# dV of head pair 0: GpSimd's rows as 16 KB packets instead of 8 KB

## The chip, the cores and the metric

The kernel runs on one core of a Trainium2 chip. The metric is device time in microseconds (us). Before the change the median of three runs is 633.36 us (632.92 to 633.75). A profiled execution is a separate run, with its own time: 632.87 us.

## The reference: what is computed

Attention of one query row per head over 8192 keys, forward and backward, in bfloat16, for 32 heads of size 128:

```python
scores = einsum('bhqd,bhkd->bhqk', q, k) * Dh**-0.5     # B=1, H=32, Sq=1, Skv=8192, Dh=128
attn   = softmax(scores, axis=-1)
out    = einsum('bhqk,bhkd->bhqd', attn, v)
out, vjp = jax.vjp(that, q, k, v);  return out, *vjp(grad_out)
```

The outputs are `out` and `dq` (8 KB each), `dk` and `dv` (64 MB each). With one query row, dK is an outer product of the row dS and q, and dV of the row P and grad_out. K and V are read (134 MB), dK and dV written (134 MB).

## The kernel before, in words

The heads are taken two at a time: 16 pairs. A pair's K is a tile of 128 partitions (64 per head) by 128 slots by 128 elements: 32 KB in each partition, 4 MB in all, and the same for V. Partition p holds 128 consecutive rows of the sequence, so its 32 KB are contiguous in memory too. There are three buffers for K and two for V. dK and dV are written in place over K and V (`outer`, line 285, on the vector engine, in eight parts of 16 slots), and the tiles are then stored to `out_2` and `out_3`. A buffer is loaded again only when its store has landed.

The loop over j runs through the pairs. It finishes dK of pair j-1, makes the scores and the softmax of pair j, and writes dV of pair j; the order of the instructions on each engine is the program's (`tc.manual_schedule`).

All loads of K and V and nearly all stores are issued from SP's queue, in the program's order, one DMA of 128 partitions each, so that each of the 16 DMA engines gets 8 rows of it. Pair 0's V is the exception on the way out. Line 299 stores its upper 64 slots from SP. Its lower 64 slots (`SHARED = 64`; 128 rows of 16 KB, 2 MB) are stored from GpSimd's queue by `share_out` (line 115), as soon as the fourth part of dV is written (line 296). `share_out` cuts the 128 rows into six DMAs, listed in `SHARES` as (engine, first row, number of rows); each takes every third row from the first:

```python
SHARES = ((6, 12, 39), (5, 2, 42), (5, 1, 8), (15, 55, 25), (10, 25, 10), (7, 0, 4))
```

The program keeps a model of which DMA engine GpSimd's queue will begin with, `cursor`. Line 121 moves it on, after a DMA of n rows, by the largest divisor of n up to 16, as if a DMA of n rows is dealt in equal runs to that many consecutive engines. `turn_to` (line 105) issues a small DMA of a few bytes a row (`turned`, line 111) ahead of each of the six, to bring the cursor to the engine that `SHARES` names. By this model the 39 rows go three each to the 13 engines from 6 on (6 to 15, 0, 1, 2), the 42 rows three each to 14 engines from 5, the 8 rows one each to 8 engines from 5, the 25 rows five each to the 5 engines from 15, the 10 rows one each to 10 engines from 10, and the 4 rows one each to 4 engines from 7.

At the end of the program GpSimd's queue also stores the two small results (line 341): 32 rows of 256 B each.

Pair 0's V buffer is loaded with pair 2's V after both stores have landed (`load_v`, line 93).

Of the kernel before, what the change touches and what calls it, by code (L numbers as in the profile page):

```python
# [31 lines left out]
def kernel(  # L32
# [11 lines left out]
    nc = tc.nc  # L44
# [62 lines left out]
    def turn_to(engine):  # L107
        n = (engine - cursor[0]) % 16
        if n:
            rows = n if n > 1 else 17  # L110
            nc.gpsimd.dma_start(turned[0:rows, cursor[1]],  # L111
                                k[0, 0].rearrange("(p n) d -> p n d", p=P)[0:rows, 0:2, 0:2])
            cursor[1] += 1
        cursor[0] = engine

    def share_out(dst, src):
        for engine, first, n in SHARES:
            turn_to(engine)
            last = first + 3 * n - 2
            nc.gpsimd.dma_start(dst[first:last:3], src[first:last:3], max_dma_last_dim=8192)  # L120
            cursor[0] = (cursor[0] + max(i for i in range(1, 17) if n % i == 0)) % 16

    ident = consts.tile([P, P], BF16)
# [162 lines left out]
    def outer(j, which, r):  # L286
        x = st[j]
        G, dst = (Kt[j], out_2) if which == "dk" else (Vt[j], out_3)
        rep, row = x["ds"] if which == "dk" else x["p"], qd[j][:, 0 if which == "dk" else 1, :]
        nc.vector.tensor_tensor(  # L290
            slots(G, r, NU).rearrange("p n (a b) -> p n a b", b=R),
            slots(rep, r, NU).unsqueeze(2).to_broadcast([P, CH, D // R, R]),
            row.rearrange("p (a b) -> p a b", b=R).unsqueeze(1).to_broadcast([P, CH, D // R, R]),
            op=ALU.mult)
        if (which, j) == ("dv", 0):
            if (r + 1) * CH == SHARED:
                share_out(rows_of(dst, 0)[:, 0:SHARED, :], G[:, 0:SHARED, :])
            elif r == NU - 1:
                nc.sync.dma_start(rows_of(dst, 0)[:, SHARED:NT, :], G[:, SHARED:NT, :])
            return  # L300
        ends = ENDS.get((which, j), (8,))
        if r + 1 in ends:
            i = ends.index(r + 1)
            a, b = (ends[i - 1] if i else 0) * CH, (r + 1) * CH
            nc.sync.dma_start(rows_of(dst, j)[:, a:b, :], G[:, a:b, :])
# [49 lines left out]
    for j in range(HP + 1):  # L355
# [30 lines left out]
        if j == 0:  # L386
            blocks(1)
            first = psT.tile([P, 512], F32, tag="T", name="first")
# [136 lines left out]
```

## Time and profile before

| | |
|---|---|
| median of three runs | 633.36 us (632.92 to 633.75) |
| profiled execution, its own time | 632.87 us |
| its span, first to last instruction | 631.1 us |
| vector engine busy | 516.4 us (82%) |
| TensorE busy | 462.9 us (73%) |
| moved by DMA | 268.98 MB in 12164 packets, mean 426 GB/s |
| GpSimd's queue (q0) | 800 packets, 2.12 MB |
| SP's queue (q1) | 11232 packets, 266.34 MB |

The profile is one execution. Times in it are in microseconds from the start of the span. A packet is one contiguous piece that one DMA engine moves; each of the 16 engines moves its packets one after the other. The trace holds for each packet its queue, start, duration and size, but not the number of its engine. "DMA share" is the mean busy share of the 16 engines; it can be a little over 1, since one packet's record begins some nanoseconds before the record of the packet ahead of it ends.

### The profile page before, as it was taken

What the parts mean: (1) busy time and instruction counts of PE and PEld (TensorE: products, weight loads), DVE (VectorE), ACT (ScalarE), POOL (GpSimd) and SP (SyncE); (2) the same over time, 40 slices, a digit from 0 to 9 for tenths busy, and PEclk for the clock granted to TensorE, in tenths of its full rate; (3) what the DMA queues carried; (4) which work ended last, traced back from release to release, by engine and by line L of the source; (5) the groups of instructions that cost most, each with busy time, mean ns of one, the idle gap of its engine ahead of it and who ended that gap; (6) DMA issues with size and microseconds to landing.
All of it is one profiled execution on the core that took longest, in us unless ns stands there. A gap on an engine that the chain in (4) does not pass through costs nothing.

```text
span 631.1 us, 8018 instructions
## 1 busy us (share of the span) xinstructions
PE 462.9 (73%) x3256; PEld 245.9 (39%) x3256; DVE 516.4 (82%) x654; ACT 205.1 (32%) x460; POOL 11.3 (2%) x23
## 2 busy tenths in 40 slices
PE   4887678878787788676888757867679776697671
PEld 1443344244443425233363432624336243262441
DVE  6579997989889798796879959879697895987973
ACT  2432424043342505134052330613316142160431
POOL 2040000000000000000000000000000000000000
PEclk9789987789798977788868789777897778987785
DMA  8999999999999999999999999999999999999997
GB/s 366 433 402 436 430 428 431 429 427 440 433 427 436 436 431 433 433 432 429 429 432 429 427 433 427 433 432 418 431 430 437 436 431 425 436 427 431 428 426 336
DMA packets 12164, 268.98 MB, mean 426 GB/s; under 512 B 1856, under 2 KB 1888, under 8 KB 1888
## 3 DMA queue, kind: packets, MB, share of 16 engines
q1 hardware_dynamic: 11232, 266.34, 98.5%
q0 software_dynamic: 800, 2.12, 0.8%
q8 instruction: 25, 0.41, 0.2%
q14 instruction: 11, 0.09, 0.0%
q10 hardware_dynamic: 96, 0.02, 0.0%
HBM read 134.23 MB, written 134.23 MB: 425 GB/s over the span
## 4 chain that ended last, share of the span: by engine, by line
issue 91%; DMA 3%; PE 3%; DVE 1%; ACT 0%; POOL 0%; POOLq 0%; ACTq 0%
DMA out_dram<-Vt 2%; PE s_ps L198 1%; DMA Kt<-in_k_dram 1%; PE T_ps L215 1%; PE acc_p L265 0%; DVE XK_sb L188 0%; DVE Vt L290 0%; POOL out_dram L120 0%; DVE q_blk L174 0%; ACT p_rep L452 0%; DVE sT L205 0%; ACT win L255 0%; ACT e L440 0%; POOL turned L111 0%; POOLq L520 0%
## 5 line engine op out<-in xcount | busy, mean ns | idle before, releaser
L198 PE MATMUL s_ps<-XK_sb,q_win 128*128 128x512 bf16 x512 | 152.4, 432 | 66.6 <-DVE XK_sb L188 61.3
L290 DVE TENSOR_TENSOR Vt<-p_rep,qd 128x2048 bf16<-128x2048 bf16 x128 | 154.0, 1223 | 40.1 <-PE acc_p L265 32.2
L188 DVE STREAM_TRANSPOSE XK_sb<-Kt 128x1024 f32<-128x1024 f32 x128 | 150.2, 1218 | 37.7 <-DMA Kt<-in_k_dram 35.0
L215 PE MATMUL T_ps<-ident_f,Vt 128*128 128x128 f32 x1024 | 165.4, 314 | 6.1 <-DMA Vt<-in_v_dram 6.1
L220 ACT COPY XV_sb<-T_ps 128x512 f32<-128x512 f32 x256 | 139.6, 591 | 82.6 <-PE T_ps L215 82.4
L290 DVE TENSOR_TENSOR Kt<-ds_rep,qd 128x2048 bf16<-128x2048 bf16 x128 | 149.5, 1215 | 3.2 <-PE acc_ds L265 2.8
L215 PEld LDWEIGHTS T_ps<-ident_f,Vt 128*128 128x128 f32 x1024 | 131.2, 160 | 43.8 <-issue 18.7
L198 PEld LDWEIGHTS <-q_win 128*128 128x128 bf16 x512 | 51.6, 110 | 155.6 <-issue 123.9
L265 PE MATMUL acc_p<-Vt,win 128*32 128x512 bf16 x512 | 55.9, 439 | 2.8 <-ACT win L255 2.8
L440 ACT ACTIVATE e<-sT,nbias 128x128 f32<-128x128 f32 x16 | 8.2, 515 | 150.6 <-DVE nbias L436 150.6
L265 PEld LDWEIGHTS <-win 128*32 128x32 bf16 x1024 | 23.0, 99 | 60.6 <-issue 49.4
L265 PE MATMUL acc_ds<-Kt,win 128*32 128x512 bf16 x512 | 42.7, 429 | 4.6 <-ACT win L255 4.6
L232 PE MATMUL dp_ps<-XV_sb,do_win 128*32 128x512 bf16 x512 | 34.3, 383 | 13.5 <-ACT XV_sb L220 13.5
L255 ACT COPY win<-ds 64x128 bf16<-64x128 bf16 x32 | 9.5, 296 | 106.4 <-DVE ds L327 106.2
L232 PEld LDWEIGHTS <-do_win 128*32 128x32 bf16 x512 | 14.3, 94 | 29.2 <-issue 22.5
L441 PE MATMUL m_ps<-rs,ones_f 128*128 128x1 f32 x32 | 7.5, 305 | 24.4 <-ACT e L440 24.4
L427 PE MATMUL m_ps<-ident_f,top 128*128 128x128 f32 x16 | 4.8, 300 | 23.5 <-DVE top L425 23.5
L205 DVE STREAM_TRANSPOSE sT<-s_ps 128x512 f32<-128x512 f32 x16 | 11.5, 717 | 10.7 <-PE s_ps L198 10.7
L441 PEld LDWEIGHTS m_ps<-rs,ones_f 128*128 128x128 f32 x32 | 6.2, 242 | 27.6 <-ACT e L440 27.6
L452 ACT ACTIVATE p_rep<-e,rinv 128x512 bf16<-128x512 f32 x16 | 11.5, 722 | 13.3 <-DVE rinv L450 13.3
L427 PEld LDWEIGHTS m_ps<-ident_f,top 128*128 128x128 f32 x16 | 2.1, 133 | 31.0 <-issue 25.4
L317 PEld LDWEIGHTS m_ps<-pd,ones_f 128*128 128x128 f32 x32 | 8.2, 276 | 10.6 <-DVE prod L248 9.8
(60 smaller groups left out, 158.1 us busy)
## 6 DMA issues: line engine op xcount, KB each, us to landing
Kt<-in_k_dram SPq DMA_DIRECT2D x14, 4096.0 KB, 29.1
Vt<-in_v_dram SPq DMA_DIRECT2D x14, 4096.0 KB, 29.0
out_dram<-Kt SPq DMA_DIRECT2D x13, 4096.0 KB, 25.1
out_dram<-Vt SPq DMA_DIRECT2D x13, 4096.0 KB, 32.3
out_dram<-Vt SPq DMA_DIRECT2D x5, 2048.0 KB, 16.2
out_dram<-Kt SPq DMA_DIRECT2D x5, 2048.0 KB, 15.7
Kt<-in_k_dram SPq DMA_DIRECT2D x4, 1024.0 KB, 8.2
Vt<-in_v_dram SPq DMA_DIRECT2D x2, 2048.0 KB, 17.5
```

What stands on the lines that cost most here:

```text
L188: nc.vector.transpose(XK[j, u][:].rearrange("p g w i -> p (g w i)"), slots(Kt[j], u, NU).rearrange("p g d -> p (g d)").bitcast(F32))
L198: nc.tensor.matmul(st[j]["s"][:], lhsT=q_win[:, c, at:at + P], rhs=cols[:, c // 2, c % 2], start=(u == 0 and c == 0), stop=(u == NU - 1 an ...
L205: nc.vector.transpose(sT[:].rearrange("p g r -> p (g r)"), x["s"][:])
L215: nc.tensor.transpose(T_ps[:, i, :], words[:, m * P:(m + 1) * P], ident_f[:])
L220: nc.scalar.copy(XV[j][:, b * TB:(b + 1) * TB, :], st[j].pop(("T", c))[:])
L232: nc.tensor.matmul(out[b * QD:(b + 1) * QD, :], lhsT=do_win[:, b // 2, e2, at:at + QD], rhs=cols[:, z, e2, :, b * QD:(b + 1) * QD], start= ...
L255: nc.scalar.copy(win[t * M:(t + 1) * M, :, at:at + 4], src[t * M:(t + 1) * M])
L265: nc.tensor.matmul(acc[which][b * QD:(b + 1) * QD, :], lhsT=win[:, g, at:at + QD], rhs=X[:, 4 * g:4 * g + 4, :].rearrange("p n d -> p (n d)"),
L290: nc.vector.tensor_tensor(slots(G, r, NU).rearrange("p n (a b) -> p n a b", b=R), slots(rep, r, NU).unsqueeze(2).to_broadcast([P, CH, D // ...
L317: nc.tensor.matmul(x["m"][:, 1:3], lhsT=ones_f[:], rhs=x["pd"][:], start=True, stop=True, skip_group_check=True)
L441: nc.tensor.matmul(x["m"][:, 0:1], lhsT=ones_f[:], rhs=rs[:], start=True, stop=True, skip_group_check=True)
L452: nc.scalar.activation(x["p"][:], e[:].unsqueeze(2).to_broadcast([P, NT, R]), ACT.Copy, scale=rinv[:])
```

## The change

The limit on the contiguous piece that one packet of `share_out`'s DMAs may carry goes from 8192 to 16384 bytes. A row has 16384 bytes. In the program before, the access pattern of such a DMA is n rows by 2 pieces by 4096 elements; it becomes n rows by 8192 elements.

```diff
         for engine, first, n in SHARES:
             turn_to(engine)
             last = first + 3 * n - 2
-            nc.gpsimd.dma_start(dst[first:last:3], src[first:last:3], max_dma_last_dim=8192)
+            nc.gpsimd.dma_start(dst[first:last:3], src[first:last:3], max_dma_last_dim=16384)
             cursor[0] = (cursor[0] + max(i for i in range(1, 17) if n % i == 0)) % 16
```

`SHARES`, `turn_to` and the arithmetic on `cursor` stay as they are.

## The prediction

> **What bounds the kernel now.** I read the page's head first. No engine is busy all the time (vector engine 82%), and the chain that ended last is 91% "issue", so it names no cause. Then the DMA lines:
>
> ```profile
> DMA  8999999999999999999999999999999999999997
> GB/s 366 433 402 436 430 428 431 429 427 440 433 427 436 436 431 433 433 432 429 429 432 429 427 433 427 433 432 418 431 430 437 436 431 425 436 427 431 428 426 336
> q1 hardware_dynamic: 11232, 266.34, 98.5%
> q0 software_dynamic: 800, 2.12, 0.8%
> q8 instruction: 25, 0.41, 0.2%
> ```
>
> The 16 DMA engines are the bound: 98.5% and 0.8% of their time is spent on packets. Next the table by stretches (columns: stretch, its length, the five engines' busy time, PE clock, DMA share, GB/s):
>
> ```profile
> 0.00:2.00 2.00, 0.00 (x0) 0.00 (x0) 0.58 (x4) 0.34 (x1) 1.43 (x9) 1.00 0.27 45
> 2.00:36.00 34.00, 24.05 (x145) 12.84 (x145) 21.29 (x32) 13.10 (x33) 6.03 (x9) 0.90 1.00 417
> 36.00:46.00 10.00, 6.91 (x70) 3.12 (x66) 8.15 (x16) 2.54 (x7) 2.40 (x5) 0.85 1.01 411
> 46.00:62.00 16.00, 12.75 (x84) 6.52 (x76) 14.88 (x15) 4.01 (x8) 0.40 (x1) 0.99 1.02 430
> 62.00:110.00 48.00, 34.85 (x268) 18.99 (x269) 40.61 (x53) 18.46 (x42) 0.00 (x0) 0.89 1.01 432
> 110.00:620.00 510.00, 384.32 (x2701) 204.40 (x2700) 430.56 (x540) 166.55 (x372) 0.52 (x1) 0.83 1.00 431
> 620.00:626.00 6.00, 0.00 (x0) 0.00 (x0) 0.31 (x1) 0.04 (x1) 0.52 (x1) 0.50 1.04 438
> 626.00:631.00 5.00, 0.00 (x0) 0.00 (x0) 0.00 (x0) 0.00 (x0) 0.00 (x0) 0.50 0.34 144
> ```
>
> From 2 to 626 us the share is 1: no engine ever waits for work. It breaks off only in the last stretch, where engines run out one by one. Each engine's end is therefore its start plus the sum of its own packets, and the kernel ends with the engine that has most to do. In the packet records the last completion packets of SP's queue, one for each engine, lie between 626.38 and 629.86 us, mean 627.98; the span ends 1.24 us after the last, at 631.1, and the execution's time is 1.77 us more.
>
> So what counts is how GpSimd's 128 rows are spread over the engines. The view of issues, and GpSimd's order of time:
>
> ```profile
> out_dram<-Vt POOLq DMA_DIRECT2D x1, 672.0 KB, 12.2
> out_dram<-Vt POOLq DMA_DIRECT2D x1, 624.0 KB, 9.1
> out_dram<-Vt POOLq DMA_DIRECT2D x1, 400.0 KB, 21.3
> ...
> 32.13 0.65 POOL L120 DMA_DIRECT2D out_dram<-Vt  x1 [27.97 <-DVE Vt L290]
> ...
> 41.53 0.56 POOL L120 DMA_DIRECT2D out_dram<-Vt  x1 [4.61 <-DMA out_dram<-Vt]
> 42.16 0.73 POOL L111 DMA_DIRECT2D turned<-in_k_dram  x1
> 45.80 0.59 POOL L120 DMA_DIRECT2D out_dram<-Vt  x1 [2.91 <-DMA out_dram<-Vt]
> ```
>
> The third line, 25 rows, takes 21.3 us to land though it is smaller than the two above it: few engines with many packets each. The packet records say how many. q0's 800 packets are 256 of 8192 B, 32 of 512 B, 96 of 8 B and 416 of 4 B. Fourteen DMAs with 16 completion packets each make 224 of the 416. The other 192 are placeholders: an engine that gets no rows of a DMA gets a 4-byte packet for each packet that the others move. By the model of line 121 the 16-k idle engines get (3x6)+(2x6)+(8x2)+(11x10)+(6x2)+(12x2) = 192. The numbers of engines in the model thus hold: 13, 14, 8, 5, 10 and 4.
>
> **The change, part by part.**
>
> Packets. 256 packets of 309 ns become 128 of 16384 B; SP's packets of that size take 611 ns. A row costs 0.611 instead of 0.618 us. An engine has 0 to 12 rows, so it gains 0 to 0.09 us.
>
> Turns between the queues. The records show the engines taking one packet of q0, one of q1, and so on. With 16 KB packets GpSimd's rows take a larger part of 36 to 46 us, in which pair 1's V still comes in packets of 8 KB. Of q0's 79.5 engine-us of 8 KB packets about 54 were moved by 46 us; if all are, V lands at most (79.5-54)/16 = 1.6 us later. Between issued and landed, SP's queue holds 3.3 to 3.8 MB at its shortest in this part (at 53 and 65 us), 7.8 us of work at 430 GB/s. The delay disappears in that: 0.
>
> Issue and waits. GpSimd issues as many DMAs as before (557 to 682 ns each) on an otherwise idle engine. Its two waits, 4.61 and 2.91 us, are for its own first DMAs; what is queued behind them is its last two share DMAs, a turning one, and much later the results at 617.74 us. If they land sooner, the waits shorten and pair 2's V can be asked for sooner; SP's queue has work then: 0. SP's queue and ACT's get nothing new.
>
> The dealing. This is where the price can lie. The issue records write the shares as a pattern of two dimensions, [2, 39] of 8192 B, and the turning DMAs so too, [2, 6] of 4 B. With a row in one piece the share has a plain list, [39, 1] of 16384 B. The only lists on GpSimd's queue before are the results, [32, 1] of 256 B, and their packets look different: 16 of 512 B for each, two rows in one packet on each of 16 engines, while each row of a turning DMA has a packet of its own. I take it that a list is dealt in equal runs over all 16 engines from the first, the number of rows divided by 16 and rounded up, and that the cursor has no say. No row with a list of other than a multiple of 16 rows exists, so the ends are: nothing (dealt as now), and this whole step.
>
> By the model the rows now are: engines 0, 1, 2 and 15 have 12, 3 has 6, 4 has none, 5 has 4, 6 has 7, 7 to 9 have 8, 10 has 9, 11 and 12 have 8, 13 and 14 have 7. In rounded-up runs they would be 3, 3, 1, 2, 1, 1 rows on as many engines as that takes: engines 0 to 3 get 11, 4 to 7 get 10, 8 and 9 get 9, 10 and 11 get 8, 12 gets 7, 13 gets 3, 14 and 15 none. Engine 4 gains 10 rows, 5 six, 3 five, 6 three. Engine 4 pays 10 x 0.611 = 6.11 us and loses 28 placeholders of 9 ns, 0.25 us, at most. No view tells which of the sixteen ends is engine 4's. It ended at 626.38 at the earliest, so at 632.2 now, 2.4 us behind the old last end; at the latest 6.1 us behind. I take the middle, 4.3 us: 632.87 + 4.3 = 637.2 by the profiled execution, which lies 0.49 us under the median; by the median 637.7 us.
>
> The Trainium skill's page "DMA: Bandwidth & Descriptors", section "Why a DMA increments its semaphore by 16 and not by 1", has both: as a rule a DMA runs on the largest number up to 16 that divides its slowest dimension (the 192 placeholders agree), but some direct copies of GpSimd's queue were seen on 16 engines with the rows divided by 16 and rounded up on each. It does not say which copies. By the rule alone the sum would be 633.3 us, by the exception 637.7 us.
>
> **The rivals.**
>
> Steering kept. The list is dealt by its 39, 42, 8, 25, 10, 4 rows just as now. For it: the number of rows is in the pattern either way, and line 121 counts rows, not pieces. Against it: the results' packing. The gain is the 0 to 0.09 us of the packets: 633.3 us. This is the case that ends on the other side, not slower.
>
> A new deal that relieves the last engine. If the rows are dealt otherwise, but so that the engine now last loses rows and none takes its place, the end moves at most to the mean of the sixteen, 1.88 us earlier: 631.5 us. It decides once the last engine loses four rows (2.4 us) and no engine that now ends within 1.3 us of it gains more than one. The deal above can't do it: engine 4 would have to end by 623.8 us now, and none ends before 626.38.
>
> V starved. If pair 1 stood still for the 1.6 us and SP's queue ran dry, the end would move by that: 635.0 us. Against it stand 7.8 us of work in the queue.
>
> **How the numbers follow.** The new deal 0.67, since the only list that the trace shows is packed otherwise than the two-dimensional patterns, against no row that shows one steered; steering kept 0.24; relief 0.06; V starved 0.03. This kernel's runs spread by 0.13%, so 0.2% (1.3 us) is about what can be told from no change. Slower 0.70, same 0.24, faster 0.06. The likeliest case's own range is 635.8 to 639.5 (2.4 and 6.1 us on the median). To leave out no more than 2 in 10 the range takes in the steered case, from 632.7 to 639.6.
>
> **What would show it.** In both cases 128 packets of 16384 B on q0. Steered: 96 placeholders, and 320 packets of 4 B in all. Dealt anew: another number of placeholders, the 25-row DMA landing well under 21.3 us, and engines running out one by one over far more than 3.5 us, since two that had 12 and 7 rows have none and end 4 to 7 us sooner while one ends later. In 626 to 631 us the DMA share then isn't 0.34 with an end at 630 but a low tail beyond it. The stretch from 110 to 620 us should keep its share of 1.00. Wrong would be a stall in that stretch, or a wait of SP's queue for pair 1's V.

## The result and the profile after

The changed kernel takes 638.93 us (median of five runs, 638.88 to 639.27) against 632.92 us beside it (632.25 to 633.75): 1.0094 times as long, 95% interval 1.0079 to 1.0109. It is slower by 6.0 us, where 4.3 was forecast as the likeliest. The profiled execution takes 639.00 us, its span is 637.2.

First the DMA part of the page after, with the packets and queues, and the view of issues:

```profile
GB/s 364 429 410 437 429 431 431 431 421 436 435 429 428 431 431 430 439 428 429 431 433 432 431 432 427 429 428 433 435 437 431 428 429 431 432 438 429 417 387 215
q1 hardware_dynamic: 11232, 266.34, 97.5%
q0 software_dynamic: 528, 2.12, 0.8%
...
out_dram<-Vt POOLq DMA_DIRECT2D x1, 672.0 KB, 10.9
out_dram<-Vt POOLq DMA_DIRECT2D x1, 624.0 KB, 8.1
out_dram<-Vt POOLq DMA_DIRECT2D x1, 400.0 KB, 14.1
```

The rate is what it was until the last three of the 40 slices: 417, 387, 215 where before they were 428, 426, 336. SP's queue moves the same 11232 packets. GpSimd's queue has 528 packets instead of 800. By size they are 128 of 16384 B, 32 of 512 B, 96 of 8 B and 272 of 4 B. Without the 224 completion packets that leaves 48 placeholders. Steered dealing would leave 96. Runs of n/16 rounded up leave (3x3) + (2x3) + (8x1) + (3x2+1) + (6x1) + (12x1) = 48: the number of engines without a row, times the rows that the others get, DMA by DMA (the 25 rows leave one engine with one row instead of two). The 25 rows land in 14.1 us instead of 21.3: they now run on 13 engines instead of five, and in longer packets (in deal8 below, 26 rows on 13 engines in packets of 8 KB land in 16.9).

The end, in the table by stretches (stretch, its length, five engines' busy time, PE clock, DMA share, GB/s):

```profile
46.00:62.00 16.00, 12.95 (x88) 6.59 (x80) 15.12 (x14) 4.01 (x8) 0.00 (x0) 0.97 1.02 433
62.00:80.00 18.00, 13.78 (x100) 7.56 (x99) 15.83 (x23) 7.26 (x17) 0.00 (x0) 0.81 1.01 431
610.00:626.00 16.00, 9.43 (x72) 5.53 (x67) 12.82 (x19) 3.38 (x12) 1.00 (x2) 0.61 0.83 350
626.00:631.00 5.00, 0.00 (x0) 0.00 (x0) 0.00 (x0) 0.00 (x0) 0.00 (x0) 0.50 0.89 375
631.00:637.00 6.00, 0.00 (x0) 0.00 (x0) 0.00 (x0) 0.00 (x0) 0.00 (x0) 0.50 0.04 19
```

In the last stretch the share is 0.04: less than one engine of 16 works. The packet records say it outright. Fifteen engines have their last completion between 630.57 and 630.98 us, and one at 635.85. Before, the sixteen lay between 626.38 and 629.86. One engine, which has 6.0 us more to do, sets the end. While it does so the others wait: between 610 and 626 us the records show 43 engine-us of idle engines (the idle times of the 16 engines added up), where before there were none. The line of the kernel before for that stretch:

```profile
610.00:626.00 16.00, 7.80 (x50) 4.89 (x50) 9.41 (x9) 2.16 (x9) 1.04 (x2) 0.50 1.01 429
```

### The profile page after: what moved, and what is told of

Its sections match the earlier page's. It is cut to its first block, busy times and chain, and to the rows that moved or that the text cites. A ratio compares the mean times of both kernels' runs of the same rounds, so it can differ in the third digit from the quotient of the medians.

```text
span 637.2 us, 8018 instructions
## 1 busy us (share of the span) xinstructions
PE 467.5 (73%) x3256; PEld 248.4 (39%) x3256; DVE 516.5 (81%) x654; ACT 205.1 (32%) x460; POOL 10.7 (2%) x23
## 3 DMA queue, kind: packets, MB, share of 16 engines
q1 hardware_dynamic: 11232, 266.34, 97.5%
## 4 chain that ended last, share of the span: by engine, by line
issue 91%; PE 3%; DMA 3%; DVE 1%; ACT 0%; POOL 0%; POOLq 0%; ACTq 0%
DMA out_dram<-Vt 2%; PE s_ps L198 1%; DMA Kt<-in_k_dram 1%; PE T_ps L215 1%; PE acc_p L265 0%; DVE XK_sb L188 0%; DVE Vt L290 0%; DVE q_blk L174 0%; ACT p_rep L452 0%; DVE sT L205 0%; POOL out_dram L120 0%; ACT e L440 0%; ACT win L255 0%; POOL turned L111 0%; POOLq L520 0%
## 5 line engine op out<-in xcount | busy, mean ns | idle before, releaser
L198 PE MATMUL s_ps<-XK_sb,q_win 128*128 128x512 bf16 x512 | 155.5, 440 | 67.2 <-DVE XK_sb L188 62.1
L215 PE MATMUL T_ps<-ident_f,Vt 128*128 128x128 f32 x1024 | 167.7, 317 | 7.2 <-DMA Vt<-in_v_dram 7.2
L215 PEld LDWEIGHTS T_ps<-ident_f,Vt 128*128 128x128 f32 x1024 | 133.3, 162 | 45.6 <-issue 19.2
L265 PE MATMUL acc_p<-Vt,win 128*32 128x512 bf16 x512 | 57.3, 451 | 2.9 <-ACT win L255 2.9
L265 PE MATMUL acc_ds<-Kt,win 128*32 128x512 bf16 x512 | 41.2, 415 | 4.6 <-ACT win L255 4.6
L184 ACT COPY do_win<-do_cols 64x4 bf16<-64x4 bf16 x32 | 6.6, 206 | 16.1 <-PE dp_ps L232 15.9
## 6 DMA issues: line engine op xcount, KB each, us to landing
out_dram<-Kt SPq DMA_DIRECT2D x13, 4096.0 KB, 25.9
```

Of the source, the lines that this page charges most:

```text
L198: nc.tensor.matmul(st[j]["s"][:], lhsT=q_win[:, c, at:at + P], rhs=cols[:, c // 2, c % 2], start=(u == 0 and c == 0), stop=(u == NU - 1 an ...
L215: nc.tensor.transpose(T_ps[:, i, :], words[:, m * P:(m + 1) * P], ident_f[:])
L265: nc.tensor.matmul(acc[which][b * QD:(b + 1) * QD, :], lhsT=win[:, g, at:at + QD], rhs=X[:, 4 * g:4 * g + 4, :].rearrange("p n d -> p (n d)"),
```

## The experiments

Four theories were at stake. *Dealing*: a plain list of rows on GpSimd's queue is dealt in equal runs over all engines from the first, so that the engine that the program's model calls 4, which the steering gave nothing, gets ten rows. *Long packets*: 16 KB packets on GpSimd's queue cost the time by themselves. Two more came up on the way, *lateness* and *placement*. The medians of the kernel before beside the runs were 632.74 us (deal8, list8, dose5, steer16), 633.17 (steer8late, steer16p6, even16, share80) and 633.14 (the rest).

**deal8: the same dealing with short packets.**

```diff
-SHARES = ((6, 12, 39), (5, 2, 42), (5, 1, 8), (15, 55, 25), (10, 25, 10), (7, 0, 4))
+SHARES = ((0, 12, 39), (0, 2, 42), (0, 1, 8), (0, 52, 26), (0, 25, 9), (0, 0, 4))
```

> Packets stay at 8 KB in two-dimensional patterns, as in the kernel before; only the list SHARES is changed, so that every DMA begins at engine 0 and the engines get the rows that the changed kernel is thought to give them: 11 on engines 0 to 3, 10 on 4 to 7, 9 on 8, 8 on 9 to 12, 3 on 13, none on 14 and 15 (26 and 9 rows in place of 25 and 10, since 25 goes to five engines only). Theory of the dealing: engine 4 has 10 rows more than before, 10 x 0.618 = 6.2 us, so about 639 us. Rival, that the longer packets cost the time: no long packets here, so 632.9 us as before.

638.69 us, ratio 1.0094 (1.0079 to 1.0109). Fifteen engines end between 630.73 and 630.87 us, one at 635.56. Its last stretches:

```profile
626.00:631.00 5.00, 0.00 (x0) 0.00 (x0) 0.00 (x0) 0.00 (x0) 0.00 (x0) 0.50 0.88 372
631.00:637.00 6.00, 0.00 (x0) 0.00 (x0) 0.00 (x0) 0.00 (x0) 0.00 (x0) 0.50 0.04 19
```

They are nearly those of the changed kernel, with no long packet on GpSimd's queue. The dealing alone gives the whole loss.

**list8: lists of short packets.**

```diff
-            nc.gpsimd.dma_start(dst[first:last:3], src[first:last:3], max_dma_last_dim=8192)
+            for c in range(2):
+                nc.gpsimd.dma_start(dst[first:last:3, 32 * c:32 * c + 32], src[first:last:3, 32 * c:32 * c + 32])
```

> 8 KB packets as plain lists: each share goes as two DMAs of n rows by 4096 elements, one for each half of the row, in place of one of n by 2 by 4096; the turning DMAs stay. Theory of the dealing, lists are dealt over all engines from the first: 10 rows on engine 4, 10 x 0.618 us, so about 639 us, with no 16 KB packet on GpSimd's queue and 96 placeholders of 4 B (twice the 48 of the changed kernel). Rival, long packets: 632.9 us.

638.87 us, ratio 1.0097 (1.0082 to 1.0112), the last engine at 635.85 us, as in the changed kernel. The queue has 416 packets of 4 B: 320 completions of its 20 DMAs and the 96 placeholders that were expected. So it is the form of the pattern that decides who gets which row, a list or two dimensions. The number of placeholders doesn't say at which engine a list begins; the time does. By the model, a list that began where `SHARES` says would give engine 4 two rows, and one that began where the turning DMAs alone leave the cursor would give it six. No engine would gain more than that over the kernel before, so the end could move by at most about 3.7 us (an estimate, 6 x 0.611). The 5.99 us ask for nearly ten rows, as lists from the first engine give. And with the dealing equal, packets of 8 and of 16 KB take the same time (638.87 and 638.93 us).

**even16: 16 KB packets, eight rows on every engine.**

```diff
-        for engine, first, n in SHARES:
-            turn_to(engine)
...
-            nc.gpsimd.dma_start(dst[first:last:3], src[first:last:3], max_dma_last_dim=8192)
+        nc.gpsimd.dma_start(dst, src)
```

> No steering: pair 0's 128 rows of 16 KB go as a single list from GpSimd, one DMA, eight rows on each engine; the turning DMAs are gone. Theory of the dealing: engine 4 gets eight rows more than before, 8 x 0.611 = 4.9 us less 28 placeholders (0.2 us), so 637.6 us, between the runs with five rows (636.3) and ten (638.9). Rival, long packets: as many of them as in the changed kernel, so about 639 us; rival, that it is the number of DMAs or the turning: 632.9 us.

637.93 us, ratio 1.0078 (1.0065 to 1.0091); last engine at 634.69 us. The long packets alone would have left the changed kernel's 639, and the turning DMAs, which this run leaves out, aren't the cause either. The two intervals of the ratio just overlap; the last engine's ends, 634.69 and 635.85 us, tell the runs apart.

**dose5: five rows for engine 4.**

```diff
-SHARES = ((6, 12, 39), (5, 2, 42), (5, 1, 8), (15, 55, 25), (10, 25, 10), (7, 0, 4))
+SHARES = ((6, 12, 39), (5, 2, 42), (5, 1, 8), (0, 55, 25), (10, 25, 10), (7, 0, 4))
```

> The kernel before with one number changed: the 25 rows begin at engine 0 instead of 15, so engine 4 gets five rows instead of none, engine 15 seven instead of 12, and nothing else moves. Theory of the dealing: engine 4 ends 5 x 0.618 = 3.1 us later; if it was among the last of all before, as the changed kernel's 6.0 us say, the time is 632.9 + 3.0 = 635.9 us; if it was in the middle of the sixteen, 634.1. Rival, long packets: 632.9 us.

636.32 us, ratio 1.0057 (1.0042 to 1.0072). Fifteen engines end by 629.27 us, one at 632.82. Together the runs make a scale:

| run | rows on engine 4 by the model | last engine ends, us | later than before, us | per row |
|---|---|---|---|---|
| before | 0 | 629.86 | | |
| dose5 | 5 | 632.82 | 2.96 | 0.59 |
| even16 | 8 | 634.69 | 4.83 | 0.60 |
| deal8 | 10 | 635.56 | 5.70 | 0.57 |
| list8, after | 10 | 635.85 | 5.99 | 0.60 |

Each end is that of one profiled execution. Each row moves the end by nearly its own 0.61 to 0.62 us, from the first five on. So engine 4 was at the end of the sixteen before, or within a few tenths of a us of it, though it had none of GpSimd's rows. The trace has no numbers of engines; "4" is the number in the program's model, and the scale shows that the model's number moves the right one.

**four4: four packets of 4 KB a row, steered.** It was meant to show that the length of a steered packet is of no account.

```diff
-            nc.gpsimd.dma_start(dst[first:last:3], src[first:last:3], max_dma_last_dim=8192)
+            nc.gpsimd.dma_start(dst[first:last:3], src[first:last:3], max_dma_last_dim=4096)
```

> Four packets of 4 KB a row instead of two of 8 KB, patterns of two dimensions, steering as before. Theory of the dealing: engine 4 has no rows, so whatever a row costs the end stays: 632.9 us; the engines with 12 rows pay about 12 x 0.014 = 0.2 us (a packet costs 7 ns beside its bytes, by 2 x 309 against 611 ns). Rival, that the number or length of packets on GpSimd's queue decides: as far on the other side as the changed kernel, 627 us, or slower by as much, 639 us.

643.27 us, ratio 1.0159 (1.0142 to 1.0176). All three expectations missed. The packets take 159 ns, as short as expected. The view of issues has the 25 rows (400 KB) with their time to landing:

```profile
out_dram<-Vt POOLq DMA_DIRECT2D x1, 400.0 KB, 36.9
```

SP's waits in 40 to 110 us (in total, times, longest), and in SP's order of time the load of pair 2's V:

```profile
SPq L93 <- DMA out_dram<-Vt: 31.5, 3, 19.4
```

```profile
75.28 0.34 SPq L93 DMA_DIRECT2D Vt<-in_v_dram  x1
```

And the stretches:

```profile
46.00:62.00 16.00, 11.63 (x73) 5.86 (x71) 14.81 (x16) 4.01 (x8) 0.59 (x1) 1.00 1.03 431
62.00:80.00 18.00, 13.78 (x99) 7.61 (x99) 15.65 (x24) 7.69 (x19) 0.00 (x0) 0.81 0.78 309
```

In the kernel before, that load stands here in SP's order of time, and the last of the six share DMAs (4 rows, 64 KB, issued at 45.80 us) has this line in the view of issues:

```profile
65.04 0.34 SPq L93 DMA_DIRECT2D Vt<-in_v_dram  x1
```

```profile
out_dram<-Vt POOLq DMA_DIRECT2D x1, 64.0 KB, 17.3
```

GpSimd's queue and SP's take turns packet by packet: of the 316 packets of rows between 40 and 70 us, 285 have exactly one packet in the records that starts as they end (3 to 4 ns ahead), and it is one of SP's each time. So the smaller GpSimd's packets are, the smaller its part. The 25 rows take 36.9 us to land instead of 21.3, and the last row 74.5 us into the span instead of 60.3.

Pair 2's load of V goes into the buffer that these rows leave. Before, the last share DMA had landed at 63.1 us (45.8 + 17.3), and the load was issued at 65.0, when SP's own store of the upper half had landed too (issued at 38.8, 26.2 us to landing). The rows were early by 1.9 us. Here the load had to wait until 75.3, 10.2 us later, which is more than the 7.8 us of work that SP's queue holds at that point in the kernel before. SP's queue runs dry (share 0.78 between 62 and 80 us, 67 engine-us idle).

This is the theory of *lateness*: pair 2's V waits, engines idle, and those that the steering had put ahead lose their lead, while what they still have to do stays. The wait and the idle time are shown. The lost lead is argued, as the packets have no engine numbers. The idle time comes to 4.2 us for each engine, of the 10.4 us by which the last engine ends later. A further part is SP's packets of 32 KB, which between 80 and 250 us took 37 engine-us more in all than at their usual 1213 ns each (6 in the kernel before).

In the changed kernel the last row lands at 52.4 us and the load is issued at 65.1: being early buys nothing, as the load then still waits for SP's own store of the upper half (issued at 39.1, 25.9 us to landing).

**steer16: steered packets of 16 KB.** A row of 16 KB in one piece is a list, so a steered 16 KB packet needs rows of 32 KB, and these are complete only after the eighth part of dV.

```diff
-SHARES = ((6, 12, 39), (5, 2, 42), (5, 1, 8), (15, 55, 25), (10, 25, 10), (7, 0, 4))
+SHARES = ((6, 0, 26), (5, 26, 14), (15, 40, 5), (15, 45, 5), (15, 50, 5), (5, 55, 9))
...
+            nc.gpsimd.dma_start(dst[first:first + n], src[first:first + n], max_dma_last_dim=16384)
...
+            if r == NU - 1:
+                share_out(rows_of(dst, 0)[1:P:2], G[1:P:2])
+                nc.sync.dma_start(rows_of(dst, 0)[0:P:2], G[0:P:2])
```

> 16 KB packets in two-dimensional patterns: GpSimd stores whole rows of 32 KB of the odd partitions (64 rows, 2 MB as before, in two packets each), SP the even ones, and the engines get by the model of the cursor about half as many rows as before, each of double size: 6 on 0, 1, 2 and 15, three on 3, none on 4, two on 5, four on 6 to 13, three on 14. All of it is issued after the eighth part of dV instead of the fourth. Theory of the dealing: the steering holds and engine 4 has nothing, so 632.9 us, give or take 0.6 us for the half rows that engines 6, 10, 13 and 14 gain or lose. Rival, long packets: 128 packets of 16 KB on GpSimd's queue as in the changed kernel, so about 639 us.

642.2 us, ratio 1.0154 (1.0137 to 1.0171): slower than both theories said. The 96 placeholders of the steered dealing are there, so the steering held. SP's waits between 55 and 85 us:

```profile
SPq L93 <- DMA out_dram<-Vt: 21.1, 2, 13.4
```

and the load of pair 2's V in its order of time:

```profile
73.36 0.33 SPq L93 DMA_DIRECT2D Vt<-in_v_dram  x1
```

Again pair 2's V is late, by 8.3 us, and 28.7 engine-us lie idle between 62 and 80 us.

**steer8late: the same with 8 KB (the edit is against steer16).**

```diff
-            nc.gpsimd.dma_start(dst[first:first + n], src[first:first + n], max_dma_last_dim=16384)
+            nc.gpsimd.dma_start(dst[first:first + n], src[first:first + n], max_dma_last_dim=8192)
```

> The kernel of run steer16 (whole rows of pair 0's odd partitions, steered, issued after the eighth part of dV) with packets of 8 KB instead of 16 KB and nothing else changed. That run took 642.2 us where the dealing alone asked for 632.9. Theory of lateness: its rows land later, pair 2's load of V waits for them, SP's queue runs dry between 62 and 80 us (28.7 engine-us of idle there in its packet records), and the engines that have few of GpSimd's rows lose the lead that the steering gives them; so about 642 us again, with idle engines in 62 to 80 us. Rival, the 16 KB packets did it after all: about 633 us.

643.48 us, ratio 1.0174 (1.0158 to 1.0191). Pair 2's V is asked for at 77.7 us, and 100 engine-us are idle between 62 and 80. So it isn't the longer packets that made steer16 slow. In both runs pair 2's V is late and engines idle, as lateness says, but that is not the whole account of steer16: its 28.7 engine-us of idle time are 1.8 us for each engine, and SP's packets of 32 KB took 37 engine-us beyond their usual length between 80 and 250 us, another 2 us or so, while its last engine ends 7.7 us later than before. The two parts weren't separated. Whether the longer packets help here isn't clear: the intervals of the two ratios overlap.

**steer16p6, steer8p6, share8p6: the share at pair 6.** steer16 and steer8late, and the share of the kernel before, moved to a place where SP's queue is deeper.

```diff
-        if (which, j) == ("dv", 0):
+        if (which, j) == ("dv", 6):
...
-                share_out(rows_of(dst, 0)[:, 0:SHARED, :], G[:, 0:SHARED, :])
+                share_out(rows_of(dst, 6)[:, 0:SHARED, :], G[:, 0:SHARED, :])
...
-                nc.sync.dma_start(rows_of(dst, 0)[:, SHARED:NT, :], G[:, SHARED:NT, :])
+                nc.sync.dma_start(rows_of(dst, 6)[:, SHARED:NT, :], G[:, SHARED:NT, :])
```

(shown as in share8p6; in the other two the same three numbers change in steer16's and steer8late's lines)

> Run steer16 moved to pair 6: pair 6's dV goes out half from SP (even partitions) and half from GpSimd (odd partitions, steered, two packets of 16 KB a row), and pair 0's dV from SP alone. At pair 6 SP's queue holds 13 to 20 us of work instead of 8 to 14. Theories of dealing and lateness: 128 steered packets of 16 KB cost nothing, so 632.9 us, up to 634 for the rows' coarser grain, and no idle engines in 62 to 80 us. Rival, long packets: about 639 us.

638.18 us, ratio 1.0083 (1.0070 to 1.0096): a miss.

> Run steer16p6 (638.2 us, where 632.9 was asked for) with packets of 8 KB instead of 16 KB and nothing else changed. In that run the records show the packets between 250 and 400 us stretched: 18 us of excess over the usual length on GpSimd's queue and some 50 on SP's. Theory of placement: which rows an engine is given, or the pair they belong to, stretches them, not the length of the packets: about 638 us again. Rival, long packets: 633 us.

646.65 us, ratio 1.0211 (1.0196 to 1.0226): neither. Here the longer packets are faster by 8.5 us.

> The kernel before with its whole share, unchanged (8 KB, every third row, issued after the fourth part of dV), moved from pair 0 to pair 6. If the rows' placement made runs steer16p6 and steer8p6 slow, this is 632.9 us with unstretched packets; if the pair did, as loads and stores lie otherwise there, it is up to 638 us with stretched packets between 250 and 400 us.

639.57 us, ratio 1.0095 (1.0070 to 1.0121): slow too, so it isn't how those two runs cut the rows. In all three a load of V waits about 20 us for the rows (the longest such wait there is 5.4 us in the kernel before), here in share8p6, SP's waits between 250 and 330 us:

```profile
SPq L93 <- DMA out_dram<-Vt: 26.1, 2, 20.7
```

The idle time is small at 16 KB (5.5 engine-us between 200 and 400 us) and large at 8 KB (102 in steer8p6, 23 in share8p6). But between 250 and 400 us the packets of 32 KB on SP's queue also take longer than their usual 1213 ns, by 52 engine-us in all in steer16p6, 73 in steer8p6 and 59 in share8p6, where the kernel before has 11. The stretching wasn't explained. What is shown is that pair 6 is no better a place for the share.

**contig: rows in consecutive runs.**

```diff
-SHARES = ((6, 12, 39), (5, 2, 42), (5, 1, 8), (15, 55, 25), (10, 25, 10), (7, 0, 4))
+SHARES = ((6, 0, 39), (5, 39, 42), (5, 81, 8), (15, 89, 25), (10, 114, 10), (7, 124, 4))
...
-            nc.gpsimd.dma_start(dst[first:last:3], src[first:last:3], max_dma_last_dim=8192)
+            nc.gpsimd.dma_start(dst[first:first + n], src[first:first + n], max_dma_last_dim=8192)
```

> The kernel before with the 128 rows cut into consecutive runs (0 to 38, 39 to 80, 81 to 88, 89 to 113, 114 to 123, 124 to 127) instead of every third row; engines, numbers of rows and packets of 8 KB stay. Theory of the dealing alone: 632.9 us, since each engine has as many rows as before. Theory of placement: the packets of both queues stretch between 36 and 62 us, and the time rises by 1 to 4 us. The length of packets has no part in it.

632.78 us, ratio 0.9995 (0.9986 to 1.0005). At pair 0 it makes no difference which rows an engine gets, only how many. *Placement* falls there.

**share80: an attempt at a faster kernel.**

```diff
-SHARED = 64
+SHARED = 80
-SHARES = ((6, 12, 39), (5, 2, 42), (5, 1, 8), (15, 55, 25), (10, 25, 10), (7, 0, 4))
+SHARES = ((6, 12, 39), (5, 2, 42), (5, 1, 8), (15, 55, 25), (10, 25, 10), (15, 0, 4))
...
+            nc.gpsimd.dma_start(dst[first:last:3], src[first:last:3], max_dma_last_dim=10240)
```

> An attempt at a faster version: GpSimd takes 80 of pair 0's 128 slots (rows of 20 KB in two packets of 10 KB, steered as before), SP 48; the last four rows begin at engine 15 instead of 7. Engine 4, which has none of GpSimd's rows, loses 8 x 4 KB of SP's, about 8 x 0.15 = 1.2 us. Theory of the dealing: if engine 4 alone was last, 631.7 us; the records of the kernel before show a second engine ending within 0.01 us of the last and a third within 0.3 us, so the gain is more likely 0 to 0.8 us: 632.1 to 632.9 us. If pair 2's V is held up by the later issue (after the fifth part of dV instead of the fourth), slower.

636.3 us, seven of the eight runs between 633.44 and 642.04, ratio 1.0051 (1.0020 to 1.0082): slower and unsteady. In its profiled execution (641.3 us) pair 2's V is asked for at 73.2 us, and the share dips as in the other late runs:

```profile
62.00:80.00 18.00, 13.78 (x99) 7.62 (x99) 15.76 (x24) 7.26 (x17) 0.00 (x0) 0.81 0.87 355
```

This was the one attempt, and no version faster than the kernel before was found.

## Why the prediction was right

*The bound.* The end is the sum of the packets of the engine with most to do: right. One engine ends 6.0 us later, and the time rises by 6.0.

*The dealing.* The list goes in runs of n/16 rounded up from the first engine, and the cursor has no say: right. The 48 placeholders and list8 show the form, deal8 that this dealing gives the loss.

The ground in the trace that the prediction named was weak, though, and that it pointed the right way was luck. It set the results' packets, two rows in one, against turning DMAs whose rows each have a packet of their own. But 32 rows over 16 engines are two on each by either rule. And each turning DMA has 16 packets of 8 B however few its rows (96 for 21 rows in the kernel before), so most of these are placeholders. In steer16 a turning DMA of 17 rows, in two dimensions, has 16 packets of 136 B: all 17 rows of 8 B in one packet, and a placeholder as long on each engine without rows. Small rows share a packet in both forms.

The Trainium skill's page "DMA: Bandwidth & Descriptors", section "Why a DMA increments its semaphore by 16 and not by 1", has this dealing as an exception for some direct copies; the runs agree, and here the copies it holds for are the plain lists (48 placeholders). For the patterns of two dimensions its rule of the largest divisor holds (192).

*The price.* The mechanism was right and one term mis-sized: engine 4's end. No view told which of the sixteen ends was its own, and the middle was taken, 4.3 us. It was at the last, as the scale shows, and 10 x 0.611 = 6.1 us counted nearly in full: 5.99.

The result lies near the top of the range, which holds it because it reached to the latest end. The prediction's own numbers held a hint that it didn't use. By the model an engine's rows go from none to 12, 7.4 us apart, and yet the ends lay within 3.5 us. With all other packets equal, engine 4 would have ended some 4.9 us (8 rows, the mean) before the mean of 627.98, at about 623.0, and no engine ended before 626.38. So engine 4 had more of other packets than the rest, by some 6.8 us above the mean if it ended last (an estimate, 629.86 less 623.0), and a list that gives it nothing looks like the counterweight. What those packets are stays open. The 25 instruction packets of 16 KB (q8, 23.9 us together) may be among them, but the trace doesn't say on which engines they lie.

*The packets.* 0 to 0.09 us: list8 and the changed kernel differ by 0.06, within the spread of their runs.

*Turns, issue, waits.* Their price of nothing was right for packets that grow: 36 to 62 us keeps its full share, and pair 2's V is issued 0.1 us later than before. Turned round, with packets that shrink, the change costs 10 us (four4): the last row is through at 74.5 us, pair 2's V waits, and the queue is empty before it comes. The margin before that load is held up was 1.9 us, from the landing of the last share DMA to the load, and behind it stood the queue's 7.8 us, which the prediction named. The prediction looked at rows that land sooner and didn't ask how much later they may land.

*What would show it.* The number of placeholders, the quicker landing of the 25 rows and a low tail beyond 631 us came as told; from 110 to 620 us the share stays 1.00 to two digits, although the idle time begins at 610. One sign did not come: the engines that lost rows were to end 4 to 7 us sooner. They end together with the others at 630.6 us. SP's last store is issued at 624.7 us instead of 620.3; they run out of work ahead of it and wait. A DMA over 128 rows lands when the last of its engines is through, so one engine's lag can hold up the loads, the vector engine's work and the stores of all. The vector engine's last group begins 4.4 us later (615.51 us instead of 611.13), which fits.

*The rivals.* Steering kept: refuted by the 48 placeholders. Relief of the last engine: refuted, it got the most. V starved: no stall between 36 and 610 us.

## What to carry to other kernels

Where the DMA engines are busy from end to end, the time is the load of the busiest one, and an edit is judged first by which engine gets its packets; here their length mattered only where it made the rows land late (four4). The trace's smallest packets, the placeholders, tell how a DMA was dealt. A pattern that loses a dimension can change the dealing though it moves the same bytes. Ahead of any edit that makes a transfer land later, look up who waits for it and by how much it is early: here 1.9 us, and then 7.8 us of queued work.

## What the runs showed of the hardware that was not expected

- An engine without rows in one of GpSimd's two-dimensional DMAs still takes a 4-byte packet for each packet of the others: 192 in the kernel before, 96 with 16 KB steered packets (steer16). Where the rows are a few bytes and joined into one packet, the placeholder is as long as that packet (8 B and 136 B in the turning DMAs).
- A list of 39 rows is dealt three to an engine from the first on, whatever ran before it; a pattern of 39 by 2 goes on from where the cursor stands. The small turning DMAs, still issued in the changed kernel, do nothing there.
- With one packet of each queue in turn, the length of GpSimd's packets sets how fast its rows land while SP's queue is full: the 25 rows took 36.9, 21.3 and 14.1 us at 4, 8 and 16 KB. The last of these is dealt to 13 engines instead of five, so the three are not a pure scale of length; 26 rows on 13 engines at 8 KB took 16.9 us (deal8).
- Left open: why SP's packets are stretched by tens of engine-us after a late share (37 between 80 and 250 us in four4, 52 to 73 at pair 6), and what a steered 16 KB packet would give for pair 0 at its usual time. A row of 16 KB in one piece is a list, so this was not tried.
